# Talking-heads attention and a squared-ReLU FFN on one core: a first batch relaid out three chunks at a time, w_in in larger pieces, FFN units of 128 tokens, and two head pairs a visit

## The chip, the cores and the metric

The kernel runs on one NeuronCore of a Trainium2 chip. The metric is the device time of one launch in microseconds (us). The kernel before takes 605.43 us (median of three runs, 604.56 to 605.51).

## The reference

```
scores = 1/8 * q @ k^T                      # 8 batches, 12 heads, 448 queries, 64 wide
scores = einsum('bhij,hg->bgij', scores, w_pre)    # heads are mixed
attn   = softmax over the keys
attn   = einsum('bhij,hg->bgij', attn, w_post)     # mixed once more
x      = attn @ v, heads side by side: 3584 tokens x 768
out    = max(x @ w_in, 0)^2 @ w_out                # 768 -> 2048 -> 768, float32 out
```

## The kernel before, in words

**The engines.** TensorE (PE) does the products, VectorE (DVE) and ScalarE (ACT) share the evictions of PSUM, GpSimd (POOL) scales the second mixing matrix, squares the FFN's hidden values and issues the loads that cast float32 to bfloat16, SyncE (SP) issues everything else that moves.

**One batch.** Its 448 query rows are cut in four blocks: block 0 holds the last 64 rows, blocks 1 to 3 hold 128 each (row 3p + j of the first 384 stands on partition p of block j + 1). A block's scores lie with queries on partitions, one PSUM bank a head (`score`, L465 for block 0, L470 for the others); DVE or ACT casts each bank to the tile `snat`. In blocks 1 to 3 the two heads of a pair are products of 64 rows each, which stand in the upper and the lower half of the PE array.

The heads can only be mixed by a product if they stand on partitions. So a DMA on SP (`relayout`, L498) turns ten queries of `snat` with their twelve heads into a **chunk** of 120 partitions by 448 keys, `sch`. There are 45 chunks a batch: 6 in block 0, 13 in each other block, the first of which takes the two rows that the blocks before have left over. One product with `wmix` mixes a chunk (L563); then follow the row minimum on DVE (L568, signs are turned), the exponential on ACT (L571), a reciprocal on DVE (L577), the scaled second mixing matrix `wq` on POOL (L580), four products `at` that mix again and turn keys to partitions (L587), and one cast to `atb` on DVE or ACT. When half a batch has its chunks, `av` multiplies with v (L623) and ACT copies the result to `xt` (L633).

**The FFN** runs over pairs of batches in **units** of tokens, `UNITS` = 0:128, 128:384, 384:640, 640:896. A unit's first product is L668, ACT takes the ReLU (L681), POOL squares (L684), the second product is L700, DVE evicts (L715), SP stores (L724). Unit 0 needs the first half of the even batch, 128:384 its second half, 384:640 the first half of the odd batch and the last 64 rows of the even one, 640:896 the rest.

**The order** of all instructions is computed when the kernel is built. A planner (`Planner.run`) walks through time with fixed costs, takes for each engine the ready operation of the lowest number `pri`, and the result is written out as each engine's in-order queue. A chunk's `pri` is its number, relayouts and scores stand `AHEAD` = 7 chunks before it, FFN operations have a million added, so that they fill what attention leaves. A change from one PE tiling to another costs 95 ns in the plan (`TURN`). The eight PSUM banks are shared by kinds, at most (`MOST`) 4 for scores and transposes ("g"), 3 mixes ("m"), 2 "a", 2 FFN ("f"), and 6 for all that is not FFN.

**The first batch.** k, the last 64 rows of q (`qt`) and q are loaded in three to eight pieces, then v. k, q and `qt` are turned by PE in batches 0 and 1 (L353, L381) and by DMA later. The loads of w_in (L775, six, `max_dma_last_dim=1024`) are issued by POOL behind the `wq` of chunks 0, 1, 2, 4, 6 and 8, those of w_out (L814, four) behind chunks 17, 20, 23 and 26, and batch 1's q and k behind chunks 11 and 14. FFN unit 0 comes into play when all chunks of the batch's first half (0 to 19) are done.

Of the kernel before, what the change touches and what calls it, by code (L numbers as in the profile page):

```python
# [14 lines left out]
DMODEL = H * D  # L15
# [8 lines left out]
NJ = 3  # L24
# [18 lines left out]
AHEAD = 7  # L43
ROWS, COLS = 1, 2
TURN = 95
STAY = 2
SLACK = {"PE": 200, "SP": 800, "POOL": 100}
MOST = {"m": 3, "a": 2, "f": 2, "g": 4, "mix": 6}
# [10 lines left out]
UNITS = [(0, 128), (128, 384), (384, 640), (640, 896)]  # L59


class Op:
    def __init__(self, engs, lat, pri, fn, deps, bank, frees, mode):
        self.engs, self.lat, self.pri, self.fn = engs, lat, pri, fn
        self.bank = bank if isinstance(bank, list) else [bank] if bank is not None else []
        self.frees, self.mode = frees, mode
        self.left, self.next, self.at, self.eng, self.ns = 0, [], None, None, 0
        for d in deps:
            if d is not None:
                self.left += 1  # L70
                d.next.append(self)


class Planner:
# [7 lines left out]
    def add(self, eng, ns, pri, fn, deps=(), lat=60, bank=None, frees=None, mode=0):  # L82
        op = Op(eng if isinstance(eng, dict) else {eng: ns}, lat, pri, fn, list(deps), bank, frees, mode)
        self.ops.append(op)
        return op

    def run(self):
# [22 lines left out]
        t, mode = 0, 0  # L110
        while True:
            for eng, heap in ready.items():
                if busy[eng] > t:
                    continue
                kept, short, first = [], False, None
                while heap:
# [5 lines left out]
                    if not fits(op) or (short and op.bank and not wide and op.bank[0][0] == "g"):  # L122
# [44 lines left out]
            while events and events[0][0] == t:  # L167
                op = heapq.heappop(events)[2]
                if op is None:
                    continue  # L170
# [20 lines left out]
def kernel(  # L191
# [65 lines left out]
    for x in range(2):  # L257
        load_tail(0, x)
    for h0 in range(0, H, 4):
        load_kv(ks, k, 0, h0, h0 + 4)  # L260
        if h0 == 0:
            masks.make_identity(nc, ident[:, :])
    for h0 in range(0, H, 4):
        load_q(0, h0, h0 + 4)
# [32 lines left out]

    def copy(eng, out_, in_):
# [10 lines left out]

    def keep(key, fn):  # L310
# [8 lines left out]
    def load(nbytes, pri, fn, deps):  # L319
        if len(loads) >= 7:  # L320
            deps = list(deps) + [loads[-7]]
        op = add("POOL", 700, pri, fn, deps)
        done = add("LOAD", nbytes / 230.0, len(loads), lambda: None, [op], lat=6000)
# [17 lines left out]
    def t_qk(b, p):  # L341
# [27 lines left out]
        at = p - 5 if b == 0 else pri + 3  # L369
# [4 lines left out]
    def t_tail(b, g):  # L374
# [14 lines left out]
        pri = b * NCHUNK - 19 + 3 * g  # L389
# [68 lines left out]
    def score(b, r, p):  # L458
        i, at_ = slot_of(b, p)
        sn = snat[(b * (NJ + 1) + r) % 2]  # L460
        tag = "mfa"[p % 3] if b == 0 and r == 0 else "g"
        keys = [(tag, "s", b, r, p, x) for x in range(1 if r == 0 else 2)]

        def tail(slot):
            nc.tensor.matmul(slot[:, 0:S], lhsT=zt[:, p, :], rhs=kt[i][:, :, at_, :], start=True, stop=True)  # L465

        def pair(*got):
            for x, slot in enumerate(got):
                half = slice(64 * x, 64 * x + 64)
                nc.tensor.matmul(  # L470
                    slot[:, 0:S], lhsT=qz[i][half, r - 1, at_, :], rhs=kt[i][half, :, at_, :], start=True,
                    stop=True,
                )

        pri = b * NCHUNK + C0[r] - AHEAD - 0.6 - (0.7 if r == 0 else 1.4) * (NPAIR - p)
        n = b * (NJ + 1) + r - 2
        old = list(relay_of[n]) if n >= 0 else []
        ins = ready[b, p][r] + ([ready_tail[b, p]] if r == 0 else [])
        mm = score_ops[b, r, p] = add(
            "PE", 190, pri, keep(keys, tail if r == 0 else pair), ins + old, lat=200, bank=keys, mode=ROWS * (r > 0),  # L480
        )
        for x, key in enumerate(keys):
            def evac(eng, key=key, h=p if r == 0 else 2 * p + x):
# [7 lines left out]
    ring, side, src_of = [], {}, {}  # L491

# [4 lines left out]
    def move(n, pri, ns, deps, outs, srcs, lat):  # L497
        op = add("SP", ns, pri, lambda: nc.sync.dma_start(out=outs, in_=srcs), deps)  # L498
        done = add("DMA", ns / 2, pri, lambda: None, [op], lat=lat)
# [3 lines left out]
    def relayout(b, c):  # L503
        r, cc = block_of(c)
        n = b * NCHUNK + c
        blk = b * (NJ + 1) + r
        sn, sn0 = snat[blk % 2], snat[(blk - 1) % 2]
        lat = 5500 if b == 0 and c else 4500
        here = relay_of.setdefault(blk, [])
        deps = list(scopy[b, r])  # L510
        pri = n - AHEAD
        if r == 2 and cc == 0:
            src_of[n] = schl
            here.append(move(n, pri, 700, deps + side.get(b - 1, []), schl[24:96, :], sn[120:126, :, :], lat))
            return
# [12 lines left out]
        for of, r0, r1, srcs in parts:  # L528
            ns = 770 if r1 - r0 > 90 else 500
            relay_of[of].append(move(n, pri, ns, deps + old, src_of[n][r0:r1, :], srcs, lat))  # L530
        if r == 0 and cc == 5:
            here.append(move(
                b * NCHUNK + C0[2], pri + 0.5, 500, deps + side.get(b - 1, []),
# [3 lines left out]
    def places(b, c):  # L537
        r, cc = block_of(c)
        rest, first = (0, NS) if b % 2 else (P_ROWS, 0)
        if r == 0:  # L540
            return [(0, rest + CI * cc, 0, CI)]
# [9 lines left out]
    def chunk(b, c):  # L551
        n = b * NCHUNK + c
# [8 lines left out]

        def f_m(slot):
            nc.tensor.matmul(  # L563
# [30 lines left out]
        def f_ac(eng):  # L594
            for half, x0, s0, w in where:
                copy(
                    eng, atb[half][:, :, :, x0:x0 + w].rearrange("p j g m -> p (j g) m"),
# [3 lines left out]
        m = m_op[n] = add("PE", 190, n, keep(mk, f_m), relay[n] + [at_op.get(n - NE), w_ready], lat=200, bank=mk)  # L601
# [6 lines left out]
        old = [av_op[b - 1, half, g] for half in {u[0] for u in where} for g in range(3)] if b > 0 else []  # L608
# [3 lines left out]
    def av(b, half, g):  # L612
        nx = (XA, XB)[half]
        to = spans(b % 2, half)
        key = ("g", "v", b, half, g)
# [267 lines left out]
```

## Time and profile before

| what | value |
|---|---|
| median of three runs | 605.43 us |
| the profiled execution, its own time | 606.62 us |
| its span | 604.8 us |
| mean granted PE clock | 0.968 |
| busy: PE, DVE, ACT, POOL | 571.2, 489.7, 468.4, 325.6 us |
| first mixing product | 18.01 us |
| last `av` of batch 0 begins | 93.59 us |
| last `av` of batch 7 begins | 557.26 us |
| last FFN product of the chain ends | 599.9 us |

Busy time says how long an engine had an instruction in flight. A lone matmul is shown with its whole latency, so a busy PE need not be a PE at full rate; the rate is read from rows with several matmuls behind one another. "Idle before, releaser" names what an engine waited for last. The chain of work is followed back from the last instruction to what released each step.

### The profile page before, as it was taken

The numbers are of one execution on the slowest core, as the hardware profiler recorded it, in microseconds if no ns is written. First come the engines' busy times: TensorE is split into PE (matmuls) and PEld (weight loads), VectorE is DVE, ScalarE is ACT, GpSimd is POOL, SyncE is SP. The second block draws the span as 40 slices with busy tenths as digits, with TensorE's granted clock in tenths as the row PEclk, the third lists the DMA queues.
The fourth block names the chain that finished last, engine by engine and source line by source line (L and its number), as shares of the span: only waits on it lengthen the run. The fifth ranks groups of instructions, "written<-read, shape, count | busy, mean of one in ns | idle before, by whom it ended". The sixth has DMA issues, their size and how long they took to land.

```text
span 604.8 us, 16567 instructions
## 1 busy us (share of the span) xinstructions
PE 571.2 (94%) x5517; PEld 405.6 (67%) x5517; DVE 489.7 (81%) x1237; ACT 468.4 (77%) x1223; POOL 325.6 (54%) x595
## 2 busy tenths in 40 slices
PE   4678889999999999999999999999999999999996
PEld 2335646666767857675867867686777867687873
DVE  4777987879898998989799998999899989887011
ACT  2677888878889898898898878899888887985320
POOL 5353816733665727662774727672783644472530
PEclk9757999979999999999999999999999999999999
DMA  9799989974498539974597439964797426321011
GB/s 135 119 227 168 205 158 162 191 135 111 116 150 199 147 82 169 196 148 115 123 169 178 129 91 187 170 151 114 149 190 152 131 83 144 97 92 29 27 53 52
DMA packets 138222, 82.29 MB, mean 136 GB/s; under 512 B 59672, under 2 KB 134680, under 8 KB 138136
## 3 DMA queue, kind: packets, MB, share of 16 engines
q1 hardware_dynamic: 86744, 58.42, 37.9%
q0 software_dynamic: 51392, 22.81, 30.6%
q8 instruction: 43, 0.70, 0.5%
q14 instruction: 43, 0.35, 0.2%
HBM read 45.62 MB, written 11.01 MB: 94 GB/s over the span
## 4 chain that ended last, share of the span: by engine, by line
PE 86%; DVE 5%; DMA 5%; issue 2%; POOL 2%; ACT 1%; DVEq 0%; POOLq 0%; ACTq 0%
PE bank L700 24%; PE bank L668 23%; PE bank L587 13%; PE bank L563 11%; PE bank L623 7%; PE bank L470 6%; DMA sch<-snat 4%; PE bank L465 2%; DVE mn L568 2%; DVE snat L300 1%; DVE atb L300 1%; POOL wq L580 1%; DMA qt<-in_q_dram 1%; PE bank L353 0%; POOL w L775 0%
## 5 line engine op out<-in xcount | busy, mean ns | idle before, releaser
L571 ACT ACTIVATE es<-bank,mn 120x448 bf16<-120x448 f32 x360 | 229.5, 644 | 33.8 <-DVE mn L568 27.2
L580 POOL TENSOR_SCALAR wq<-wback,rc 120x120 bf16<-120x120 f32 x360 | 130.8, 367 | 211.9 <-DVE rc L577 128.9
L568 DVE TENSOR_REDUCE mn<-bank 120x1 f32<-120x448 f32 x360 | 211.0, 611 | 5.9 <-PE bank L563 5.1
L700 PE MATMUL bank<-w,h 128*128 128x384 bf16 x896 | 174.5, 326 | 0.1
L300 DVE CAST atb<-bank 112x480 bf16<-112x480 f32 (+3 forms) x235 | 142.9, 619 | 36.5 <-PE bank L587 33.4
L668 PE MATMUL bank<-xt,w 128*128 128x256 bf16 (+1 forms) x1536 | 163.8, 259 | 0.0
L587 PEld LDWEIGHTS <-es 120*112 120x112 bf16 (+1 forms) x1440 | 120.8, 134 | 46.2 <-issue 20.7
L668 PEld LDWEIGHTS <-w 128*128 128x128 bf16 x1536 | 133.2, 98 | 25.2 <-issue 5.0
L587 PE MATMUL bank<-wq,es 120*112 120x120 bf16 (+1 forms) x1440 | 132.2, 222 | 14.1 <-POOL wq L580 12.6
L684 POOL TENSOR_TENSOR h<-hr 128x512 bf16<-128x512 f32 x112 | 116.5, 1041 | 48.5 <-ACT hr L681 46.6
L700 PEld LDWEIGHTS <-h 128*128 128x128 bf16 x896 | 83.0, 97 | 55.3 <-issue 6.7
L563 PE MATMUL bank<-sch,wmix 120*128 120x448 bf16 x352 | 115.1, 365 | 3.6 <-DMA sch<-snat 3.1
L302 ACT CAST snat<-bank 128x448 bf16<-128x448 f32 x174 | 88.0, 540 | 19.3 <-PE bank L470 10.5
L300 DVE CAST snat<-bank 128x448 bf16<-128x448 f32 x162 | 96.1, 614 | 2.7 <-PE bank L470 1.8
L681 ACT ACTIVATE hr<-bank 128x512 f32<-128x512 f32 x112 | 67.1, 599 | 34.2 <-PE bank L668 29.0
L302 ACT CAST atb<-bank 112x480 bf16<-112x480 f32 (+2 forms) x149 | 78.7, 537 | 19.0 <-PE bank L587 17.6
L571 ACT ACTIVATION_READ_ACCUMULATOR es<-bank,mn 120x1 f32 x360 | 75.7, 210 | 0.0
L577 DVE RECIPROCAL rc<-sm 120x1 f32<-120x1 f32 x360 | 53.5, 154 | 18.6 <-ACT es L571 16.5
L715 DVE COPY osb<-bank 128x384 f32<-128x384 f32 x56 | 30.9, 552 | 39.5 <-PE bank L700 39.5
L470 PE MATMUL bank<-kt,qz 64*128 64x448 bf16 x288 | 50.9, 372 | 2.1 <-DVE qz L300 1.8
L563 PEld LDWEIGHTS <-wmix 120*128 120x128 bf16 x360 | 32.4, 99 | 21.3 <-issue 9.2
L623 PE MATMUL bank<-atb,vs 112*64 112x192 bf16 (+1 forms) x768 | 43.8, 275 | 0.0
(45 smaller groups left out, 228.0 us busy)
## 6 DMA issues: line engine op xcount, KB each, us to landing
sch<-snat SPq DMA_DIRECT2D x336, 105.0 KB
out_dram<-osb SPq DMA_DIRECT2D x23, 360.0 KB
vs<-in_v_dram POOLq DMA_DIRECT2D x16, 336.0 KB, 8.7
ks<-in_k_dram POOLq DMA_DIRECT2D x14, 336.0 KB, 9.0
qs<-in_q_dram POOLq DMA_DIRECT2D x14, 288.0 KB, 8.7
w<-in_moe_w_in_dram POOLq DMA_DIRECT2D x6, 512.0 KB, 20.0
w<-in_moe_w_out_dram POOLq DMA_DIRECT2D x4, 768.0 KB, 17.5
out_dram<-osb SPq DMA_DIRECT2D x8, 192.0 KB
```

Source lines behind the costliest of these rows:

```text
L300: nc.vector.tensor_copy(out=out_, in_=in_)
L302: nc.scalar.copy(out=out_, in_=in_)
L470: nc.tensor.matmul(slot[:, 0:S], lhsT=qz[i][half, r - 1, at_, :], rhs=kt[i][half, :, at_, :], start=True, stop=True,)
L563: nc.tensor.matmul(slot[:, 0:S], lhsT=wm[0:rows, :], rhs=src[0:rows, :], start=True, stop=True,)
L568: nc.vector.tensor_reduce(out=mn[i][0:rows, :], in_=slots[mk][0:rows, 0:S], axis=AX.X, op=ALU.min)
L571: nc.scalar.activation(out=es[i][0:rows, 0:S], in_=slots[mk][0:rows, 0:S], func=ACT.Exp, scale=-1.0, bias=mn[i][0:rows, 0:1], accum_out=sm ...
L580: nc.gpsimd.tensor_scalar(out=wq[i][0:rows, :, 0:ns], in0=wback[0:rows, :, 0:ns], scalar1=rc[i][0:rows, 0:1], scalar2=1.0, op0=ALU.mult, o ...
L587: nc.tensor.matmul(slot[0:P_KEYS, jb * H * ns:(jb + 1) * H * ns], lhsT=es[i][0:rows, jb * P_KEYS:(jb + 1) * P_KEYS], rhs=wq[i][0:rows, :, ...
L623: nc.tensor.matmul(v_[64 * hh:64 * hh + 64, i, 0:nx], lhsT=vs[:, 2 * c2 + hh, jb, :], rhs=atb[half][:, jb, 2 * c2 + hh, :], start=(jb == 0 ...
L668: nc.tensor.matmul(slot[:, j * w:(j + 1) * w], lhsT=w1[c2][:, (f0 + j) * 128:(f0 + j + 1) * 128], rhs=xt[:, c2, a:z], start=(c2 == 0), sto ...
L684: nc.gpsimd.tensor_tensor(out=h2_[:, f0:f0 + nf, 0:w], in0=hr[gi % 2][:, :].rearrange("p (f c) -> p f c", f=nf), in1=hr[gi % 2][:, :].rear ...
L700: nc.tensor.matmul(slot[:, 0:384], lhsT=h2_[:, ft, mt * 128:(mt + 1) * 128], rhs=w2[:, ft, nt * 384:(nt + 1) * 384], start=(ft == 0), stop ...
```

## The change

In the first batch:

- Chunks of blocks 0 and 1 (but for block 1's first) are relaid out three at a time (`triple`): one DMA brings 60 query rows of block 0, or 30 of block 1, to a tile of 120 partitions by 3 x 448, three heads side by side in each row. A chunk is then mixed by three accumulating products with three matrices `wtri` in place of one. That makes six such moves for 18 chunks. Five buffers for them are cut out of `osb` and `h2`.
- Eighteen matrices `wtri` are built by DVE or POOL at the start (`tri_one`), from `wpre_tri`: three SP loads, and twelve small ones for block 0.
- The order of the chunks is written out (`ORDER0`): block 0, block 1's twelve, block 1's first, block 2, block 3, the leftover chunk of each of the two last ahead of its twelve.
- `av` of a half is split, and the first four FFN spans of 0:384 become units of 128 (`UNITS0`): 0:128 can begin after block 1, 128:256 after block 2's rows, 256:384 at the end of the batch.
- w_in is loaded in pieces of 4096 bytes in place of 1024, straight behind q: two pieces, then v, then four; no longer behind `wq` of the first chunks. w_out is cut by rows of the hidden dimension, not by output columns.

In batches 1 to 7 the scores of blocks 1 to 3 are planned two head pairs at a time (`GROUP` = 2): four banks at once. "g" may hold 6 banks, all that is not FFN 7. While an operation of several banks lacks room, other "g" operations are held back. The planner has a new model of the two DMA queues, with rows and times a row, for its own due times.

```diff
-AHEAD = 7
+AHEAD = 7.2
+HOLD = "g"
+GROUP = 2
-MOST = {"m": 3, "a": 2, "f": 2, "g": 4, "mix": 6}
+MOST = {"m": 3, "a": 2, "f": 2, "g": 6, "mix": 7}
+LOADS0 = [("k", 0), ("t", 0), ("t", 1), ("k", 1), ("k", 2), ("q", 0), ("q", 1), ("q", 2)]
+UNITS0 = [(0, 128), (128, 256), (256, 384), (384, 640), (640, 896)]
+NTRI = 5
+TRI_IN = (0, 1)
+W2_AT = [18, 21, 24, 27]
+Q1_AT = [13, 16]
...
+    for x in range(3):
+        nc.sync.dma_start(out=wpre_tri[x][:, :], in_=w_pre[x:H:3, :].unsqueeze(0).to_broadcast([3 * CI, H // 3, H]))
...
+    for y in range(3):
+        for x in range(2):
+            for g in range(2):
+                nc.sync.dma_start(
+                    out=wpre_tri[3 + y][2 * x + g:KC:4, :],
+                    in_=w_pre[6 * g + 2 * y + x:6 * g + 2 * y + x + 1, :].to_broadcast([3 * CI, H]),
+                )
...
+    def tri_one(eng, m, x):
+        e_ = nc.vector if eng == "DVE" else nc.gpsimd
+        e_.memset(wtri[m][x][:, KC:P], 0.0)
+        e_.tensor_tensor(
+            out=wtri[m][x][:, 0:KC].rearrange("p (s h) -> p s h", s=CI),
+            in0=wpre_tri[m // 3 * 3 + x][:, :].unsqueeze(1).to_broadcast([KC, CI, H]),
+            in1=nmask3[:, m % 3, :].unsqueeze(2).to_broadcast([KC, CI, H]), op=ALU.mult,
+        )
+    mask_ready = add("DVE", 700, -40, tri_mask)
+    for m in [3, 4, 5, 0, 1, 2] if 0 in TRI_IN else [0, 1, 2]:
+        for x in range(3):
+            tri_ready.setdefault(m, []).append(
+                add({"DVE": 420, "POOL": 650}, 0, -20 + 0.1 * m, lambda eng, m=m, x=x: tri_one(eng, m, x), [mask_ready])
+            )
...
+            here.append(move(
+                n, pri, 800, deps + old, src_of[n][:, :, :].rearrange("k x s -> k (x s)"),
+                sn[60 * t:60 * t + 60, 0:NPAIR, :].rearrange("t (g x) s -> t g (x s)", x=3) if r == 0 else
+                sn[t:t + 4 * 29 + 1:4, :, :].rearrange("t (g x) s -> t g (x s)", x=3), lat,
+            ))
...
+            if three:
+                for x in range(3):
+                    nc.tensor.matmul(
+                        slot[:, 0:S], lhsT=wtri[sub(b, c)][x][:, :], rhs=src[:, x, :], start=x == 0, stop=x == 2,
+                    )
+                return
...
+    def groups(b, r):
+        size = GROUP if b > 0 and r > 0 else 1
+        return [range(p, p + size) for p in range(0, NPAIR, size)]
...
+    started = add("POOL", int(1000 * at_), -100, lambda: None)
+    def load_w1(c2, pri):
+        w1_in.append(load(16, 173, pri, lambda: nc.gpsimd.dma_start(
+            out=w1[c2][:, :], in_=moe_w_in[c2 * 128:(c2 + 1) * 128, 0:DFF], max_dma_last_dim=4096,
+        ), [started]))
```

`at_` is 7.65, so `started` holds POOL in the plan until 7.65 us. A `load` waits for the load seven places before it.

## The prediction

> **What bounds the kernel now.** I read the busy time by stage first, because the page's 94% for PE is a mean over unlike stages. Columns: stage in us, its length, busy time (count) of PE, PEld, DVE, ACT, POOL, granted clock, DMA share, GB/s.
>
> ```profile
> 18.00:60.00 42.00, 31.01 (x205) 17.69 (x202) 32.30 (x83) 30.40 (x84) 18.87 (x37) 0.63 1.08 177
> 60.00:95.00 35.00, 28.70 (x380) 20.95 (x379) 30.03 (x78) 28.83 (x77) 16.04 (x32) 1.00 0.98 176
> 95.00:560.00 465.00, 463.01 (x4534) 332.85 (x4533) 412.96 (x1041) 395.30 (x1041) 267.71 (x496) 0.99 0.67 138
> 560.00:600.00 40.00, 39.90 (x302) 29.20 (x300) 4.47 (x9) 8.94 (x15) 14.55 (x14) 1.00 0.16 43
> ```
>
> From 95 to 560 us PE never rests (463 of 465). Up to 95 us no engine is full, but the DMA engines are (shares about 1), and PE's clock is 0.63 for 42 us. The last 40 us are FFN alone: two units of 256, of which the chain shows 10.48 + 10.40 = 20.9 us for one. Only one of them needs the last `av`; the other is backlog. So PE time that is saved or used earlier shortens the end one for one up to 20.9 us, and beyond that only if attention itself gets faster.
>
> The chain of work (start, us, what) says what the first batch waits for:
>
> ```profile
> 26.53 8.52 DMA sch<-snat
> ...
> 37.04 8.87 DMA sch<-snat
> ```
>
> Two relayouts hold it for 17 us. At that time POOL has issued w_in, and the queues from 20 to 40 us (packets, MB, share of 16 engines) are
>
> ```profile
> q0 software_dynamic: 3978, 2.01, 79.1%
> q1 hardware_dynamic: 1777, 1.47, 31.1%
> ```
>
> A load packet is 505 B and holds an engine 79.1% x 20 us x 16 / 3978 = 64 ns; a relayout's of 896 B holds it 56 ns. w_in in bfloat16 is 3.15 MB, some 6144 such packets: 6144 x 64 / 16 = 24.6 us of all engines, and that is where the relayouts queue.
>
> **Score visits.** This PE timeline (start, us, line, tile) shows the price of a head pair between other work:
>
> ```profile
> 377.33 0.54 PE L563 MATMUL bank<-sch,wmix 120*128 120x448 bf16 x2
> 377.80 0.36 PE L470 MATMUL bank<-kt,qz 64*128 64x448 bf16 x2
> 378.10 0.36 PE L563 MATMUL bank<-sch,wmix 120*128 120x448 bf16 x1
> ```
>
> Two mixes of 448 columns behind one another step by 0.187 us (0.54 minus one latency of 0.35), so the pair could start at 377.70 and starts at 377.80; a pair whose halves run at once needs 0.187 too, and the next starts 0.30 after it. A visit loses 0.10 going in and 0.11 coming out, 0.20 us. Over 95 to 560 us I counted 101 visits in the PE timeline, 83 of one pair and 18 of two, for 119 pairs. Two at a time make it 60. **41 x 0.20 = 8.2 us less**, in a stage where PE is the bound. Ends: 8.2 saved and, where order separates the two pairs or their banks come late, nothing; I take 8.2, as a visit now is one operation of the planner.
>
> **Three products.** 18 chunks take two more products of 0.187 us: 6.7 us of PE, all in the first batch; twice that at half clock. It lies in PE time that is idle today; I count it against the room for FFN below.
>
> **The start.** This part speaks against the change. 18 matrices are built in the plan right after the mask, with no word of when their inputs arrive: DVE does 17 by 0.76 + 17 x 0.42 = 7.9 us, the last falls to POOL at 7.65. Nine need the twelve small SP loads. DVE's queue is in order, so everything planned after 7.9 us, the first `zt`, `kt` and `snat` evictions, stands behind builds that wait for SP. What SP pays for one issue is shown here (start, us), and for the stores as min/median/max in ns:
>
> ```profile
> 0.75 1.00 SPq L268 DMA_DIRECT2D wpre_rep<-in_w_pre_dram  x1
> 1.80 0.78 SPq L269 DMA_DIRECT2D wpost_rep<-in_w_post_dram  x1
> ...
> L724 SPq DMA_DIRECT2D out_dram<-osb x58: 450/584/845, 113.2 to 601.4; - x58
> ```
>
> Fifteen more, at 0.45 to 0.78 plus a gap of 0.08, are issued by 2.6 + 8.0 = 10.6 or 2.6 + 12.9 = 15.5 us. The first relayout gives about 2.3 us from the end of an issue to the product that needs it (14.90 + 0.78 to 18.01), so the last input is there at 12.9 to 17.8; six builds of 0.37 (two take 0.67 today, and a memset) end at 15.1 to 20.0. In the profile before DVE reaches that point here:
>
> ```profile
> 8.36 0.36 DVE L300 COPY zt<-bank 128x384 bf16<-128x384 bf16 x1 [2.09 <-PE bank L381]
> ```
>
> So the first evictions come 6.7 to 11.6 us later, unless the loads come sooner than either row says: then nothing. From `zt` to the first relayout takes 6.5 us today, with k already there later a little less. **I take +7: the first mixing product at 25 us in place of 18.** POOL's one build holds the issue of w_in and v likewise, to some 16 us, still ahead of the first `wq`.
>
> **From the first product to the batch's last `av`.** Today 18.01 to 93.59, 75.6 us. Later batches, whose relayouts find the queue free, put like `av`s 65.5 us apart ((557.26 - 164.44) / 6); with 3 us for filling the pipe, 68.5. Three things take the first batch there: w_in goes out before the first relayout, not beside it; larger pieces hold the engines shorter (between the 24.6 us by bytes and 1536 x 64 / 16 = 6.1 by packets; the planner's own 173 ns give 16.6); and six moves in place of 18 mean one wait for three chunks. The DMA-issue steps that the chain shows on POOL (0.93, 0.88 and 0.88 us for w_in) leave it as well. Next late is DVE with ACT: 413 and 395 busy us in 95 to 560 are (413 + 395) / 2 / 7 = 58 us a batch. Ends: 0 and -14.6 (58 + 3); I take **-7**, the pace that the trace shows. With the start, the batch ends at 93.5, as it does now.
>
> On the move itself one rule speaks against a gain. The Trainium skill, "DMA: Bandwidth & Descriptors", section "Why small descriptors are slow (HBM only)", says that transfers within SBUF do not suffer from small descriptors. By it three chunks in rows of 2688 B cost the queue what three chunks in rows of 896 B do; no row of before has the larger size. Its result is the third case below.
>
> **FFN earlier.** Until 93.6 us the FFN has had 96 products of L668 and 16 of L700, 5.4 + 2.6 = 8 us. After the change unit 0:128 is free after 19 chunks, 128:256 after some 32: 21 us of work. PE needs of 25 to 93.5, 68.5 us: mixes 45 x 0.187 = 8.4, the extra 6.7, `at` 180 x 0.052 = 9.4, 18 pairs at 0.30 = 5.4, `av` 4.8, and for batch 1 turns, scores and first mixes some 9: 44. Room 24.5, of which about 10 lie before the 19th chunk, when no unit is free. So 14.5 us of FFN in place of 8: **-6.5**. Ends: -13 (both units) and 0. The rest of the diff (order, other shares of `av`, w_out by rows, q and k of batch 1 at other steps, buffers in `osb` and `h2`) moves issues between queues that have room; 0, with +-2 in the range.
>
> **Sum**, against the execution's own 606.62 (its span and 1.8 around it): -8.2 + 7 - 7 - 6.5 = -14.7, so 591.9. The median lies 1.2 below that execution: **590.7 us**.
>
> **The rivals.**
> - *The weights come in time* (SP issues them faster than its rows, or ACT has the early evictions): the +7 goes, 583.7. For it: SP has nothing else until 14.9. Against: no SP row is below 0.45. Chance 0.17.
> - *The first batch pays and does not get faster*: the 7 of the pace are not gained, since the DMA engines stay full and three chunks in one move take as long as three moves. 597.7. The skill's rule above would give this. For it: w_out, v, and q and k of batch 1 still share the queue with blocks 2 and 3, which today run 1.6 us a chunk too. Chance 0.2.
> - *Banks*, on the other side. A visit needs four free banks at once, holds other scores back, and leaves the FFN one bank where it had two. If PE stands for one eviction (0.58 us, `snat` on DVE 0.61 and ACT 0.54) at each of 63 visits, that is 36.5 us: 627. It decides from 14.7 / 63 = 0.23 us a visit. For it: DVE is 89% busy from 95 to 560. Against: attention has work for other banks then, and FFN backlog is long. Chance 0.13. The Trainium skill, "TensorEngine Tiling (Array Packing)", section "Gotcha 1: PSUM Pressure", points the same way: row tiling raises the pressure on PSUM, as the row tiles write to different banks; no row of before shows a bank lacking.
> - *The change does not do what it says*: the two pairs are parted or were mostly neighbours in cost, and visits save nothing: 590.7 + 8.2 = 598.9. Chance 0.05.
>
> **The numbers.** The forecast has 0.45. The range goes from 577 (early weights and both units within the batch, 583.7 - 6.5) to 605 (no faster pace, late end of the start's bounds, 597.7 + 4.6, and the +-2); above it lie most of the bank case and a little of the third. About 0.2% (1.2 us) is what a measurement of this kernel can tell from no change. Faster: nearly all of the forecast and of early weights, most of the third and last cases, a tenth of the bank case, 0.83. Slower: the bank case, 0.12. Same: 0.05.
>
> **What would show it.** First mixing product near 25 us, with DVE's builds of `wtri` waiting for a DMA before it (near 18: the second case). Last `av` of batch 0 near 93 and no relayout wait above 4 us before it. FFN products of 14 us or so before that point. Some 63 visits in batches 1 to 7, PE still busy from 95 to the end, attention's last `av` at 545 to 552. Wrong it would be if PE shows idle time behind 95 us, by evictions or for want of FFN units.

## The result, and the profile after

| | before | after |
|---|---|---|
| median, us | 605.11 (604.56 to 605.51, 4 runs) | 608.58 (607.9 to 608.9, 4 runs) |
| ratio to before, 95% interval | | 1.0057 (1.0039 to 1.0074) |
| span of the profiled execution, us | 604.8 | 607.1 |
| first mixing product, us | 18.01 | 32.84 |
| last `av` of batch 0 begins, us | 93.59 | 108.92 |
| from there to the end of the span, us | 511.2 | 498.2 |

The kernel is 0.6% slower; 590.7 was forecast. The last three rows cut the span in three stretches, and these sum to the whole difference: to the first mix +14.8 (forecast +7), from there to the batch's last `av` +0.5 (forecast -7), behind it -13.0 (forecast -8.2 - 6.5 = -14.7). Sum +2.3, the spans' difference. The stretch behind batch 0 came out nearly as forecast; the first batch did not. The row of `av` that is read here holds the batch's last 16 products before and the last 32 after. Read at the start of the batch's last single `av` product (94.39 and 110.52), the three are +14.8, +1.3 and -13.9, so the second and the third are good to about 1 us.

The busy times by stage, in the same columns as before (stage, length, PE, PEld, DVE, ACT, POOL, granted clock, DMA share, GB/s):

```profile
0.00:18.00 18.00, 1.76 (x22) 1.31 (x22) 5.48 (x43) 2.73 (x4) 8.07 (x18) 1.00 0.72 79
18.00:60.00 42.00, 32.78 (x237) 16.08 (x237) 32.43 (x80) 28.42 (x70) 15.58 (x31) 0.92 0.83 165
60.00:95.00 35.00, 28.77 (x488) 23.55 (x489) 25.03 (x70) 26.14 (x74) 16.27 (x31) 0.95 1.03 198
95.00:560.00 465.00, 461.15 (x4643) 332.99 (x4643) 412.79 (x1051) 405.47 (x1072) 268.52 (x500) 0.99 0.69 141
560.00:600.00 40.00, 40.00 (x346) 30.32 (x344) 8.06 (x17) 12.17 (x24) 16.48 (x20) 1.00 0.09 24
```

PE does 22 products in the first 18 us; in the kernel before it was busy for 8.61 us there. From 95 to 560 us it stays full, so the banks did not become the bound. From 60 to 95 us DVE and ACT are less busy than before (25 and 26 us against 30 and 29) while the DMA share is above 1: something waits for transfers there. The longest such wait is the one that the chain below has at 91.81: the casts to `snat` stand still for it, for 4.6 us on DVE and 3.9 us on ACT.

DVE's timeline shows what the first stretch waits for (start, duration, line; in brackets the idle time before it and what ended that):

```profile
13.41 0.28 DVE L412 TENSOR_TENSOR wtail<-wpre_tail,nmask 120x120 bf16<-120x120 f32 x1 [2.00 <-DMA wpre_tail<-in_w_pre_dram]
...
14.87 0.28 DVE L412 TENSOR_TENSOR wtail<-wpre_tail,nmask 120x120 bf16<-120x120 f32 x1 [1.16 <-DMA wpre_tail<-in_w_pre_dram]
...
16.89 0.67 DVE L412 TENSOR_TENSOR wtail<-wpre_tail,nmask 120x120 bf16<-120x120 f32 x2 [1.73 <-DMA wpre_tail<-in_w_pre_dram]
...
18.30 0.34 DVE L391 COPY zt<-bank 128x384 bf16<-128x384 bf16 x1
```

DVE's part of `zt` stands at the end of the builds and comes at 18.30 (ACT casts the other part at 9.72); before, DVE's came at 8.36. The builds wait for the small loads, one group at a time. SP's own rows:

```profile
5.29 10.27 SPq L383 DMA_DIRECT2D wpre_tail<-in_w_pre_dram  x12
24.95 1.87 SPq L636 DMA_DIRECT2D osb<-snat  x2
```

Twelve issues of 30 rows each hold SP for 10.27 us. The first relayout is issued at 24.95, 6.65 us behind `zt`, as forecast. The chain of work then says (start, us, what):

```profile
24.95 7.85 DMA osb<-snat
32.84 3.53 PE bank L727 x9
37.29 7.55 DMA sch<-snat
...
91.81 2.75 DMA sch<-snat
```

That relayout takes 7.85 us to land. In the kernel before the first one gave its product 3.1 us after its issue (14.90 to 18.01); its row there is

```profile
14.90 4.91 SPq L498 DMA_DIRECT2D sch<-snat  x6
```

That move is of 105 KB, the changed kernel's of 315 KB, and in the changed kernel POOL had issued w_in and v from 17.43 to 23.28, just ahead of it.

Last, a visit with two pairs in the PE timeline:

```profile
375.58 0.55 PE L607 MATMUL bank<-kt,qz 64*128 64x448 bf16 x4
376.06 0.36 PE L731 MATMUL bank<-sch,wmix 120*128 120x448 bf16 x1
```

Four products for two pairs, and the next product starts 0.48 us after the first; two visits of one pair would take 0.30 each. Behind 110 us there are 60 visits, all of two pairs; in the kernel before 18 of 96 were. (The expectation of e1 counts 4 more of one pair and 80 in place of 78: they come from visits that the edge of a window of the timeline cuts in two.)

### The profile page after: what moved, and what is told of

It reads as the page before. It is cut to its first block, busy times and chain, and to the rows that moved or that the text cites. A ratio compares the mean times of both kernels' runs of the same rounds, so it can differ in the third digit from the quotient of the medians.

```text
span 607.1 us, 17020 instructions
## 1 busy us (share of the span) xinstructions
PE 566.8 (93%) x5745; PEld 405.4 (67%) x5745; DVE 484.7 (80%) x1259; ACT 474.9 (78%) x1240; POOL 324.9 (54%) x597
## 4 chain that ended last, share of the span: by engine, by line
PE 80%; DMA 4%; DVE 4%; POOL 3%; ACT 3%; issue 3%; SPq 2%; DVEq 0%; POOLq 0%; ACTq 0%
PE bank L848 22%; PE bank L880 22%; PE bank L755 12%; PE bank L731 10%; PE bank L795 7%; PE bank L607 6%; DMA sch<-snat 3%; SPq L383 1%; ACT es L739 1%; DMA osb<-snat 1%; POOL wq L748 1%; DVE mn L736 1%; DVE snat L391 1%; POOL h L864 1%; DVE atb L391 1%
## 5 line engine op out<-in xcount | busy, mean ns | idle before, releaser
L739 ACT ACTIVATE es<-bank,mn 120x448 bf16<-120x448 f32 x360 | 229.3, 645 | 33.1 <-DVE mn L736 26.8
L391 DVE CAST atb<-bank 112x480 bf16<-112x480 f32 (+2 forms) x221 | 134.8, 621 | 30.8 <-PE bank L755 28.4
L848 PEld LDWEIGHTS <-w 128*128 128x128 bf16 x1632 | 137.4, 98 | 22.9 <-issue 2.4
L755 PEld LDWEIGHTS <-es 120*112 120x112 bf16 (+1 forms) x1440 | 115.8, 130 | 42.2 <-issue 11.1
L755 PE MATMUL bank<-wq,es 120*112 120x120 bf16 (+1 forms) x1440 | 127.6, 218 | 9.0 <-POOL wq L748 7.7
L731 PE MATMUL bank<-sch,wmix 120*128 120x448 bf16 x334 | 104.0, 354 | 0.2
L393 ACT CAST snat<-bank 128x448 bf16<-128x448 f32 x172 | 85.2, 546 | 22.7 <-PE bank L607 15.5
L393 ACT CAST atb<-bank 112x480 bf16<-112x480 f32 (+3 forms) x163 | 88.2, 555 | 14.9 <-PE bank L755 14.1
L745 DVE RECIPROCAL rc<-sm 120x1 f32<-120x1 f32 x360 | 53.3, 154 | 17.7 <-ACT es L739 13.6
L895 DVE COPY osb<-bank 128x384 f32<-128x384 f32 x56 | 30.9, 551 | 32.4 <-PE bank L880 32.2
L607 PE MATMUL bank<-kt,qz 64*128 64x448 bf16 x288 | 42.2, 357 | 3.8 <-DVE snat L391 2.8
L795 PE MATMUL bank<-atb,vs 112*64 112x192 bf16 (+3 forms) x864 | 43.0, 260 | 0.5 <-ACT atb L393 0.5
L731 PEld LDWEIGHTS <-wmix 120*128 120x128 bf16 x342 | 29.8, 98 | 19.2 <-issue 11.1
```

Of the source, the lines that this page charges most:

```text
L391: nc.vector.tensor_copy(out=out_, in_=in_)
L393: nc.scalar.copy(out=out_, in_=in_)
L607: nc.tensor.matmul(slot[:, 0:S], lhsT=lhsT, rhs=kt[i][half, :, at_, :], start=True, stop=True)
L731: nc.tensor.matmul(slot[:, 0:S], lhsT=wm[0:rows, :], rhs=src[0:rows, :], start=True, stop=True,)
L739: nc.scalar.activation(out=es[i][0:rows, 0:S], in_=slots[mk][0:rows, 0:S], func=ACT.Exp, scale=-1.0, bias=mn[i][0:rows, 0:1], accum_out=sm ...
L755: nc.tensor.matmul(slot[0:P_KEYS, jb * H * ns:(jb + 1) * H * ns], lhsT=es[i][0:rows, jb * P_KEYS:(jb + 1) * P_KEYS], rhs=wq[i][0:rows, :, ...
```

## The experiments

Each kernel's span is read in the same cuts: first mix, last `av` of batch 0, and the rest behind it. "Told" kernels start from the changed one. The expectations name the runs e1 to e16 by their order. With the batch's last single `av` product in place of the last row of `av`, no difference that is quoted below moves by more than 1 us, but for those of e9. A split is read from one profiled execution, and the executions of a kernel differ: e2's ten run from 600.73 to 607.10 us, and its split is of the one at 600.73; e14's ten run from 601.17 to 606.50 us, and its split is of one at 606.08.

**e1, one pair a visit, new limits.** `GROUP = 2` becomes 1.

> The changed kernel with head pairs planned one at a time in all batches (GROUP = 1). Theory: the pairs are worth 8 us (the trace of the changed kernel shows 60 visits of two pairs and 4 of one behind 110 us, before 18 and 80), and the loss lies in the first batch, so this takes 616 to 617 us and its last av of batch 0 stays at 109 us. Rival: four banks at once cost more than the visits save, and that is the loss; then it takes 600 us or less.

633.94 us, ratio 1.0465 (1.043 to 1.0501). Dearer than either side said. **e7** has the old limits as well (`"g": 4, "mix": 6`):

> The changed kernel with pairs one at a time and the old bank limits (4 for scores, 6 for all that is not FFN). e1 kept the limits 6 and 7 and took 633.9 us, 25 more than the changed kernel, where 8 were expected of the visits. Theory: with single pairs the new limits starve the FFN of banks, so here most of that comes back: 613 to 617 us, the visits alone. Rival: single visits themselves cost 25 us in the new plan: 630 us or more.

619.65 us, 1.0248 (1.0225 to 1.0271). PE from 95 to 560 us in e1, then in e7:

```profile
95.00:560.00 465.00, 449.80 (x4476) 318.35 (x4475) 407.99 (x1047) 402.30 (x1065) 259.97 (x492) 0.99 0.70 138
```

```profile
95.00:560.00 465.00, 459.41 (x4624) 329.08 (x4622) 422.66 (x1071) 405.13 (x1069) 271.83 (x508) 1.00 0.70 140
```

With seven banks for attention and single pairs PE idles 15 us in this stretch, and the old limits give 14.3 us of the loss back, though 619.65 is above the 613 to 617 of the theory. That the FFN starves of banks, as the theory has it, was not shown: of the 14.0 us of waits of PE that e1's profile lists here, 11.6 end with a cast of scores or of `atb`. The rest behind batch 0 is 506.6 us in e7 and 498.2 in the changed kernel: pairs at once, with the limits that go with them, are worth 8.4 us there, 11.1 in the median.

**e4, the kernel before with two pairs.** `GROUP`, `HOLD` and the limits alone.

> The kernel before with only the two pairs at a time in batches 1 to 7, the bank limits 6 and 7, and the hold of other scores. Theory: 41 visits less at 0.20 us, 597 to 598 us against 605. Rival (banks): 605 or more.

601.09 us, 0.9932 (0.9901 to 0.9962). The part pays in the other kernel too: 4.0 us in the median, half of the 8.2. The visits behind 110 us fall from 96 to 57, as meant, but from 95 to 560 us PE now idles 4.3 us, where it idled 2.0; what the rest went to was not shown.

**e2, fewer small loads.** The twelve become six, three on SP and three on ACT:

```
-        for x in range(2):
-            for g in range(2):
-                nc.sync.dma_start(out=wpre_tri[3 + y][2 * x + g:KC:4, :], ...)
+        for g, issuer in enumerate((nc.sync, nc.scalar)):
+            issuer.dma_start(out=wpre_tri[3 + y][g:KC:2, :], ...)
```

> The changed kernel with the twelve small loads of w_pre as six, three issued by SP and three by ACT; the plan is the same. Theory: VectorE's queue stands behind builds that wait for those loads, so the last of them lands near 10.5 us in place of 16.9, the zt eviction starts near 12.5 in place of 18.3, and nearly all of that reaches the end: 602 to 604 us. Rival: the first batch is bound by what its loads and relayouts move, the earlier start is given back by the last av of batch 0, and the time stays at 607 to 609 us.

604.46 us, 0.999 (0.9968 to 1.0013), 4 us below the changed kernel. `zt` comes at 15.70 in place of 18.30, the first mix at 30.04, batch 0's last `av` at 102.09. As expected in kind, but `zt` was expected near 12.5 and the time at 602 to 604 us; the landing still takes 8.4 us (21.65 to 30.04).

**e3, the plan told.** The planner is given the times at which the weights landed in the changed kernel, so the builds are planned behind the first evictions:

```
+            there = [7600, 8200, 9900, 13400, 14900, 16900][m // 3 * 3 + x]
+            landed = add("WEIGHT%d%d" % (m, x), 0, 0, lambda: None, lat=there)
-                add({"DVE": 420, "POOL": 650}, ..., [mask_ready])
+                add({"DVE": 420, "POOL": 650}, ..., [mask_ready, landed])
```

> The changed kernel with the plan told when the inputs of the eighteen matrices arrive (7.6 to 16.9 us, as its trace shows), so that the builds stand behind the first evictions in VectorE's queue; loads as they were. Theory: zt is evicted near 9 us, the first relayout is issued near 16, the builds end near 19, the first mixing product comes at 20 to 23 us in place of 32.8: 597 to 600 us. Rival (given back within the batch): 607 to 609 us.

600.07 us, 0.9913 (0.9883 to 0.9944): no load and no build less, only their place in the queues, and 8.5 us come back. `zt` is at 9.33 (on ACT), the first mix at 23.60. But blocks 2 and 3 then take 46.1 us (54.46 to 100.55; 40.3 in the kernel before). One of e3's windows shows why:

```profile
82.00:86.00 4.00, 0.00 (x0) 0.00 (x0) 0.00 (x0) 0.00 (x0) 0.00 (x0) 1.00 0.70 176
```

and its chain, for the same place:

```profile
79.80 6.29 DMA sch<-snat
```

All engines stand still for one relayout: the casts of the next scores to `snat` wait for it, 6.6 us on DVE and 5.6 us on ACT. At 53 to 66 us POOL had issued the four loads of w_out.

**e5, w_out earlier**, `W2_AT = [2, 5, 8, 11]` upon e3.

> The kernel of e3 (plan told when the weights' inputs arrive) with w_out loaded behind steps 2, 5, 8 and 11 in place of 18, 21, 24 and 27. In e3 the queue of loads stands empty from 38 to 46 us (DMA share 0) and is full from 54 to 74, when the relayouts of blocks 2 and 3 go; from 82 to 86 all engines stand still for one of these. Theory: what the first batch gains in blocks 0 and 1 is given back there, to loads that were moved on top of the later relayouts; then the stop at 82 goes, the last av of batch 0 comes 4 to 6 us earlier than 100.6, and the time is 594 to 597 us. Rival: SP's own issuing (1.25 us a move) is what makes the late relayouts late; then 599 to 601 us.

617.88 us, 1.0217 (1.0198 to 1.0236). Both sides missed. The first `av` comes at 53.64, about as in e3 (54.46), the last of batch 0 only at 108.66, and not for want of the queue:

```profile
66.00:80.00 14.00, 8.46 (x47) 5.15 (x47) 8.86 (x21) 6.38 (x18) 5.58 (x11) 0.63 0.65 120
80.00:95.00 15.00, 14.62 (x218) 11.16 (x217) 12.13 (x31) 11.02 (x31) 5.03 (x10) 1.00 0.12 36
```

From 66 to 80 us PE and DVE are busy for some 60% and the others less, at a DMA share of 0.65, and behind 80 us the DMA engines rest: `wq` waits for `rc`, the exponential for the minimum, `at` for `wq`, chunk behind chunk. The plan has the chunks follow one another there. Clearing the queue is not enough by itself.

**e10, w_out later**, `W2_AT = [30, 33, 36, 39]` upon e3.

> e3 with the four loads of w_out behind the chunks at places 30, 33, 36 and 39 of the batch's order in place of 18, 21, 24 and 27. In e3 PE, DVE and ACT all stand still from 82 to 86 us for a relayout of blocks 2 and 3, and the last av of batch 0 is at 100.55 us. Theory (w_out's bytes hold the relayouts of blocks 2 and 3): the stop goes, the last av of batch 0 comes at 95 to 98 us, and the time falls to 595 to 598 us. Rival (it is batch 1's q and k, or SP's own issues, that hold them): the last av stays at 99 to 102 us and the time at 599 to 602 us. If the FFN's second halves want w_out earlier, PE would show idle time between 95 and 150 us and the time would rise above 602 us.

594.93 us, 0.983 (0.9802 to 0.9858). As the theory had it, and more: the last `av` comes at 92.65, 7.9 us earlier. From 60 to 95 us e3 shows the first row, e10 the second:

```profile
60.00:95.00 35.00, 28.07 (x408) 21.65 (x406) 23.41 (x63) 26.75 (x71) 15.15 (x27) 0.90 0.72 149
```

```profile
60.00:95.00 35.00, 31.41 (x502) 24.20 (x501) 30.89 (x84) 34.13 (x93) 21.17 (x38) 1.00 0.83 181
```

DVE and ACT do 7 us more work in the same 35 us, with a higher DMA share: w_out is now issued from 70.6 to 83 us, and the moves of block 2 go ahead of it. The stop is gone.

**e12, the same edit upon the changed kernel itself.**

> The changed kernel with one edit: the four loads of w_out behind the chunks at places 30, 33, 36 and 39 in place of 18, 21, 24 and 27. No arrival times are told, so the start is that of the changed kernel (first mix at 32.84 us). In e10 the same edit upon e3 moved the last av of batch 0 from 100.55 to 92.65 us. Theory (w_out's place is what took back in blocks 2 and 3 what blocks 0 and 1 had gained): the last av of batch 0 goes from 108.9 to 100 to 103 us, and the time from 608.6 to 602 to 605 us. Rival (e10's gain needs the early start, with the loads of batch 1 further from the moves): the last av stays at 106 to 109 us, the time at 606 to 609 us.

607.76 us, 1.0066 (1.0037 to 1.0095). Split: the last `av` moves to 103.09, 5.8 us earlier, but the rest takes 502.5 us in place of 498.2, so the span gains 1.5. The first half of the theory holds, its total does not.

**e9, w_in behind the first chunks** as in the kernel before, upon e3 (v stays ahead):

```
+            if n in W1_AT:                      # [0, 1, 2, 4, 6, 8]
+                load_w1(W1_AT.index(n), n, gate(n))
```

> e3 with w_in no longer issued ahead of the first relayout but, as in the kernel before, behind the weights of chunks 0, 1, 2, 4, 6 and 8 of the batch; v stays ahead. e3 took 600.07 us; its first relayout was issued at 15.86 us, landed 7.7 us later, and the first mixing product came at 23.6. Theory (the landing is long because the move stands in the DMA queues behind the loads issued ahead of it): the first relayout lands 3 to 5 us behind its issue, the first mix comes at 19 to 21 us, and the kernel takes 595 to 598 us. Rival (the queue is only filled a little later, and the same bytes sit on the moves of blocks 0 and 1 instead): the first mix comes earlier, but the last av of half 0 stays at 53 to 56 us as in e3 (54.46), and the time at 599 to 602 us.

610.85 us, 1.0098 (1.0062 to 1.0134): slower, which neither side had. Its chain, with e3's beside it in the second fence:

```profile
15.84 4.74 DMA osb<-snat
20.62 4.11 PE bank L730 x12
```

```profile
15.86 7.71 DMA osb<-snat
23.60 3.53 PE bank L729 x9
```

The landing is 3.0 us shorter, as the theory said. Batch 0 ends earlier, by 3.0 us as the rows of `av` are cut (97.53) and by 1.6 us by its last product (99.86 against 101.42). The loss lies behind it, 511.5 us in place of 497.0.

**e6, every chunk alone** (`TRI_IN = ()`: no triples, no extra weights), upon the changed kernel.

> The changed kernel with every chunk relaid out by itself: no builds of wtri, none of their fifteen loads, one product a mix; order, loads, FFN units and pairs as changed. Theory: the start is free (first mixing product at 18 to 20 us in place of 32.8) and the triple moves brought little, so that this is faster than the changed kernel by 8 us or more: 600 us or less. Rival: three chunks in one move are worth as much as the late start costs: 605 us or more.

615.01 us, 1.0166 (1.0146 to 1.0186). The first mix comes at 21.45, and then its chain shows

```profile
14.82 6.59 DMA sch<-snat
21.44 15.13 DMA sch<-snat
```

so blocks 0 and 1 take 45.5 us from the first mix to the first `av`, against 30.3 in the changed kernel. The rival held. **e11** adds e9's later w_in:

> e6 (every chunk moved alone, no extra weights) with w_in issued as in e9, behind the weights of chunks 0 to 8. e6 took 615.01 us; its first mix came at 21.45 us, was followed by a wait of 15.1 us for the second relayout, and half 0 of the batch ended at 66.97 us. Theory (w_in and v issued ahead of the moves, not the single moves as such, cost e6 its blocks 0 and 1): half 0 ends at 53 to 58 us and the time is 600 to 605 us. Rival (single moves are slow wherever the loads stand): half 0 ends at 62 us or later, and the time is 609 to 615 us.

608.22 us, 1.0057 (1.0037 to 1.0076). The same stretch takes 42.3 us (18.97 to 61.28); with triples and w_in behind (e9) it is 28.7. Between the two expectations: w_in ahead costs single moves 3 us, and single moves are slow either way. In this order, that is: the kernel before, with single moves in another order, takes 35.3. Of the 7 us between them 5.8 are relayouts on the chain (17.01 + 6.14 us in e11, 8.52 + 8.87 in the kernel before); what in the order makes them longer was not shown.

**e8, small pieces of w_in** (1024 bytes) upon e3.

> The kernel of e3 with w_in in pieces of 1024 bytes as before. Theory: w_in then holds the DMA engines up to 24.6 us in place of 6 to 17, and the relayouts of blocks 0 and 1 queue behind it: 603 to 608 us against 600. Rival: the size of the pieces does not matter, 599 to 601 us.

600.17 us, 0.9931 (0.9911 to 0.9952): no difference to e3. The queues from 20 to 40 us (packets, MB, share of 16 engines), e8 first:

```profile
q0 software_dynamic: 4822, 2.42, 89.7%
```

```profile
q0 software_dynamic: 1794, 2.45, 68.6%
```

The larger pieces do hold the engines a quarter less for the same bytes. Nothing on the path notices.

**e13, FFN units as in the kernel before**, upon e10:

```
-UNITS0 = [(0, 128), (128, 256), (256, 384), (384, 640), (640, 896)]
+UNITS0 = UNITS
```

> e10 (594.93 us) with the FFN's units of the first pair of batches as in the kernel before: 128 to 384 as one unit at the end of batch 0, in place of two of 128. Theory (the early second unit is used: in e10 the FFN has had 19.7 us of PE time by 110 us): the work by 110 us falls to 13 to 16 us, and the kernel takes 596 to 599 us. Rival (the unit of 128 changes nothing that lasts, since the FFN's backlog is long): 594 to 596 us. If smaller units cost more than they bring: below 594 us.

593.07 us, 0.9824 (0.9795 to 0.9853): the same as e10 within the intervals, and the fastest median here, by the ratio 1.8% below the kernel before, and 15.5 us below the changed one. FFN work by 110 us falls, as the theory says: PE is busy with its products for 18.3 us until then, in e10 for 23.1. Yet the time does not rise. The row from 95 to 560 us shows how it is caught up:

```profile
95.00:560.00 465.00, 464.94 (x4638) 337.71 (x4637) 405.62 (x1026) 395.96 (x1046) 272.94 (x503) 1.00 0.69 138
```

PE never rests; e10 idles 2.4 us there. And batch 0 ends 1.9 us earlier by its last `av` product (91.61 against 93.52).

**e14, six small loads on SP**, upon e10, with earlier arrivals told.

> e10 with the twelve small loads as six (two rows of the weights each), all from SP, and arrivals of 7.6, 8.2, 9.9, 11.0, 12.0 and 13.5 us told to the planner. In e10 SP issues small loads until 15.7 us, and the first relayout follows at 15.83. Theory (SP's own issues now set the first relayout): it is issued at 14 to 15 us, the first mix comes at 21.5 to 23 us in place of 23.59, and the time is 592 to 594.5 us. Rival (the relayout lands when the loads ahead of it are through, whenever it is issued): first mix at 23 to 24 us, and 594 to 596 us.

602.78 us, 0.997 (0.9944 to 0.9996). SP is done with the small loads at 10.9 us in place of 15.7, but the relayout is issued at 16.31, no earlier (e10: 15.83); batch 0 ends at 93.02, about as in e10 (92.65); the rest takes 511.3 us against 500.2, in an execution 3.3 us above the median. **e15** has the same six loads upon e13 with the told times unchanged, so the order on all engines is e13's:

> e13 (593.07 us) with the twelve small loads as six on SP, but with the arrivals told to the planner unchanged, so that the order of all engines' instructions is that of e13. e14, which changed both, lost 8 us against e10, all of it behind batch 0 (467.2 + 44.1 us from the last av of batch 0 to the end, against 461.2 + 39.0). Theory (the other order of the plan cost e14 its 8 us, not the loads): the last av of batch 0 at 88.5 to 90.5 us, from there to the end 498 to 501 us, and a time of 590.5 to 593.5 us. Rival (the six loads themselves do harm, in SP's queue or in the landing of the moves): 597 us or more.

594.79 us, 0.9848 (0.9804 to 0.9892); first mix 23.17, last `av` of batch 0 at 91.19, rest 501.7 (e13: 23.52, 90.3, 499.8). The median is 1.3 us above the expected band and the same as e13's within the intervals. The loads do no harm, so e14's loss is put down to the other order, the one thing left that e14 changes. They bring nothing either: the move issued at 15.47 still lands with the loads ahead of it.

**e16, batch 1's first loads later**, `Q1_AT = [18, 21]` upon e13.

> e13 (593.07 us) with batch 1's first loads of q and k behind the chunks at places 18 and 21 of the order in place of 13 and 16. Theory (what w_out did in blocks 2 and 3 these loads do too, on a smaller scale): the last av of batch 0 comes 1 to 3 us earlier than 90.3 us, the time is 590 to 592.5 us. Rival (they are needed by then): batch 1's turns wait, DVE and ACT have less to do between 60 and 90 us, and the time is 595 to 600 us.

601.14 us, 0.9946 (0.9925 to 0.9967). The rival is the nearer, though the time is above its band: batch 0 ends at 93.32 instead of 90.3, and the rest takes 508.4. From 60 to 90 us DVE is busy for 26.8 us and ACT for 25.8, in e13 for 27.8 and 28.1, as the rival says. In this plan the loads are better where they are.

## Why the prediction was wrong

**The start (+7 forecast, +14.8 measured): the step that failed most.** The builds in DVE's queue were foreseen, and their size was inside the bounds: DVE's `zt` 9.9 us later, where 6.7 to 11.6 had been given and 7 taken. SP's issues came 0.86 us apart (10.27 us for twelve), the upper of the two rows that were weighed; the choice near the lower end was the error. The other 4.8 us were not in the sum at all. The prediction had w_in and v go out "to some 16 us, still ahead of the first `wq`" and took the landing of the first relayout as today's. It did not ask what stands in the DMA queues ahead of that move: the relayout comes behind 5.9 us of load issues and lands in 7.85 us in place of 3.1. e3 shows the first term (builds told to come later: first mix 9.2 us earlier). The second comes apart by the time from the first relayout's issue to the first mix:

| | w_in behind | w_in ahead |
|---|---|---|
| single move, 105 KB | 3.87 (e11) | 6.63 (e6) |
| triple move, 315 KB | 4.78 (e9) | 7.75 (e3) |

w_in ahead costs 2.8 to 3.0 us, the larger move 0.9 to 1.1. The 0.75 us between e11 and the kernel before (3.12) are not told apart. So the landing was mis-sized in two ways, by the queue for the most part and by the size of the move for some.

**The pace of the first batch (-7 forecast, +0.5 measured).** The gain was there and was given back. From the first mix to the first `av` the changed kernel takes 30.3 us, the kernel before 35.3: -5.0. From there to the last `av` 45.8 against 40.3: +5.5. (The first `av` covers 19 chunks here and 20 there. To the first `at` of the 20th chunk it is 29.9 us against 33.1, so the gain by like chunks is 3.2.) Of the three things named for the gain, w_in "before the first relayout, not beside it" brings none (30.9 us with it ahead in e3, 28.7 behind in e9), larger pieces none (e8), and the six moves carry it: 42.3 us without triples, 28.7 with, w_in behind in both (e11, e9). Of those 13.6 us, though, 7.0 only make up for what e11 takes more than the kernel before; against that one's 35.3 it is 6.6. What takes it back is tied to w_out's place: e10 and e12, the same edit upon two kernels, end batch 0 earlier by 7.9 and 5.8 us, and e3's stop, which goes with it, is a wait for a relayout. The early FFN units have a share as well (e13 against e10: 1.9 us by the last `av` product). The term of w_out stood under "moves issues between queues that have room; 0". In these stages the DMA share is about 1, as the prediction's own first view showed: there was no such queue. How much of the edit's effect is bytes in the queue and how much the plan's order in blocks 2 and 3 is not told apart; e5, which cleared the queue and lost, shows that the order counts too.

**The rule that spoke against triples.** The case that "three chunks in one move take as long as three moves" did not come: the stretch to the first `av` got shorter. Whether larger rows also spare the DMA engines is another question. From 20 to 40 us the queue of the loads and that of the relayouts (q1) in the changed kernel are

```profile
q0 software_dynamic: 2677, 3.22, 94.5%
q1 hardware_dynamic: 629, 1.48, 21.0%
```

against 1777 packets, 1.47 MB and 31.1% of q1 before: the same bytes with a third less engine time. But the two kernels differ in their loads too, which share the engines. With nearly the same loads, w_in behind the first chunks, e9 (triples) and then e11 (single moves) show for q1

```profile
q1 hardware_dynamic: 723, 1.46, 26.7%
q1 hardware_dynamic: 1293, 1.07, 20.6%
```

That is 18.3% and 19.3% for a MB, and 16.1% and 16.4% where w_in is ahead (e3: 33.1% for 2.06 MB, e6: 30.4% for 1.85 MB). So with like loads larger rows spare the engines 2 to 5% for the same bytes. The Trainium skill, "DMA: Bandwidth & Descriptors", section "Why small descriptors are slow (HBM only)", has transfers within SBUF free of that penalty; these four rows agree with it nearly. What failed is the step from there to "as long as three moves": the gain of the triples lies in waits on the chain (7.55 us behind the first landing in the changed kernel and 5.75 in e9, 17.4 in the kernel before and 23.2 in e11), not in engine time for a byte.

**Score visits (-8.2).** Right, as far as it can be isolated: 60 visits of two pairs at 0.48 us, and 8.4 us of the stretch behind batch 0 between e7 and the changed kernel. e7 has 104 visits behind 110 us, so 44 at the prediction's 0.20 us would make 8.8. The limits changed with the pairs there, and up to 1.7 us are idle time of PE (5.6 against 3.9 us). Upon the kernel before it brings half (e4).

**FFN earlier (-6.5).** It failed as a step. When batch 0 ends the FFN has had 192 products of its first kind and none of the second, at the prediction's 0.056 us each 10.8 us, where 8 were had before and 14.5 forecast: 2.8 more in place of 6.5. And since batch 0 ends 15 us later there is no lead in time: PE has been busy with FFN products for 9.0 us by 95 us, against 9.1 before, and by 150 us for 37.6 against 39.9. e13 shows besides that the premise, earlier FFN work shortens the end one for one, holds only if PE has no idle time that later work can fill: 4.8 busy us less by 110 us cost nothing, as PE then idled 2.4 us less and batch 0 ended 1.9 us earlier. So the stretch behind batch 0 came near its forecast partly by chance: visits (8.4) and FFN (2.8) make 11.2 of the 13.0, and the other 2 us are not attributed. Attention's last `av` begins at 568.15, where 545 to 552 was forecast.

Together: of the 17.0 us between the forecast change of the span (-14.7) and the measured one (+2.3), the start has 7.8, the pace 7.5 and the stretch behind batch 0 1.7.

**The rivals.** The bank case did not come with two pairs: PE is busy 461 of 465 us. It came the other way round, with single pairs under the new limits (e1). "The first batch pays and does not get faster" is nearest in what happened, with a cause other than the one it named, and at 597.7 still 11 us short, for the most part by the size of the start.

**What stays open.** The stretch behind batch 0 takes 496.9 to 502.5 us in ten of the kernels with two pairs upon the changed one (the changed one among them) and 507.2 to 511.5 in the other four (e5, e9, e14, e16). Kernels with one plan agree within 2 us (498.2 and 496.9 for the changed kernel and e2; 497.0 and 497.2 for e3 and e8; 499.8 and 501.7 for e13 and e15). e14 against e15 shows that the order that the planner settles on can be worth 8 us in the median far behind the place of the edit, so an edit's total can be read only beside this split, and the totals of e9, e12 and e16 are not prices of their edits. Why some orders are worse was not settled. A part is seen: e5, e9 and e14 each have a stop of PE of 3 us, in front of an `at` (at 494.4, 486.5 and 481.8), and the ten others have none above 1 us. In e9 the chain gives it as

```profile
482.74 3.03 DMA sch<-snat
```

a relayout that is issued once a mix has released its tile, and for which the casts to `snat` wait. Shorter stops of 1.4 and 2.4 us stand near 135 (e9) and 145 us (e14). But e16 loses as much with no stop above 1.5 us.

## What to carry to other kernels

When a transfer is put ahead of another, look up what stands in the queue at the moment of the later one's issue, after all other delays of the change have been added; here loads in stages whose DMA share was about 1 were not free, and w_out, moved behind the moves that the engines wait for, ended batch 0 earlier by 5.8 and 7.9 us. A plan that is not told when its inputs arrive puts work in front of others that then wait for nothing: here the arrival times alone were worth 8.5 us. Split the time into stretches before crediting an edit, since a static order answers far from the place of the edit.

## What the runs showed of the hardware

- On SP a small load took the issue time of a larger one: twelve of 30 rows each were issued 0.86 us apart, the three of `wpre_tri`, 120 rows each, 0.88 apart.
- A stop of PE can cost more than its length. Around the stop in e9 (window, PE busy, then granted clock as the third figure from the end):

```profile
482.00:486.00 4.00, 1.58 (x14) 0.74 (x10) 0.56 (x2) 0.73 (x3) 1.36 (x2) 0.93 0.58 170
486.00:490.00 4.00, 3.46 (x14) 1.96 (x15) 3.30 (x8) 3.17 (x9) 0.73 (x2) 0.50 0.42 98
490.00:494.00 4.00, 4.00 (x25) 1.94 (x24) 2.82 (x7) 1.59 (x5) 0.26 (x1) 0.72 0.21 48
```

  3 us idle, then 4 us at 0.50 and 4 us at 0.72: another 4 x 0.50 + 4 x 0.28 = 3.1 us of PE at full clock. The Trainium skill, "TensorE: Matmul & The Clock Gate", section "Part 1: The HAM clock gate (the "warmup" mystery)", ties the granted clock to how busy PE has been of late, with half rate as the throttled one; these rows agree. The stops of 3 us in e5 and e14 are followed by 0.50 as well, but one of 2.98 us in e1 (before 224.6 us) and one of 1.36 us in e9 (before 135.8 us) by 1.00. What decides between them no run here shows.
- DMA issues on ACT ahead of its first activation delayed ACT: in e2 three of them from 0.74 us put the load of its function table at 4.28 us, in the changed kernel at 0.74. Its first copy came 0.86 us later (7.08 against 6.22).
